# Linear attention and gated MLP, two layers each: block sums of the down weights moved from the first gated MLP into the first attention layer

## The chip, the cores and the metric

The kernel runs on one core of one Trainium2 chip. The metric is the device time of the whole program in microseconds (us), as a median of separate executions; before the change it is 1495.54 us (three runs, 1492.11 to 1496.01). Durations of single instructions come from one further execution that was recorded by the hardware profiler.

TensorE (PE) does the matrix products, VectorE (DVE), ScalarE (ACT) and GpSimd (POOL) the elementwise work, and SyncE (SP) issues most of the transfers. Each engine carries out its own list of instructions in the order of that list[...].

## The reference

Two kinds of layers alternate: attention, MLP, attention, MLP. There are 2048 rows (S) of 1024 numbers (D); the MLP is 3584 wide (F).

```python
# attention layer: 32 heads of 32
qkv = layernorm(x) @ wqkv
pq, pk = phi(q), phi(k)             # t+1 or exp(t), + 1e-6
kv  = sum_s pk[s] v[s]^T ;  z = sum_s pk[s]
x  += ((pq kv) / (pq . z + 1e-6)) @ wo
# gated MLP layer
xn  = layernorm(x)
h   = relu(xn @ W_gate) * (xn @ W_up)
x  += h @ W_down
```

Both attention layers use the same weights, and so do both MLP layers.

## The kernel before

**Attention, `layer_A`.** The 16 row tiles of 128 are taken in four quarters of four tiles. A unit is one projection of one row tile onto 512 columns: 8 matmuls of 128x128 by 512 into one PSUM bank (L430). In the first layer the quarters run as 16 units of quarter 0 (`head_units`), then for q = 1 and q = 2 sixteen units each, in which k and q projections alternate, then the eight k units of quarter 3. After that come the products of the normalised rows with phi(k) (L465), the last q units, and the output units (L557). The banks of the units come from two PSUM pools: four banks of `ps` and, for every third unit outside the last quarter, two of `ps3`; a bank is free again when VectorE has read it (L380, which writes phi). Layernorm of later row tiles goes on beside the units on VectorE: two `bn_stats` of half a row (L154), an aggregate (L159) and the scaling (L168), after which SyncE issues a DMA transpose (L347).

**Gated MLP, `layer_B`.** A layer works in two chunks c of 1024 rows. The gate and up products of one unit u (256 of the 3584 columns; 14 units) are done as a 2x2 block product with seven products instead of eight. Each of the seven is four matmuls (L743), for gate and for up, so a unit has 56 matmuls. This needs sums of blocks of the rows (`sums_x`) and of the weights (`make_gu`, L677 to L680). The sums of the weights are made on VectorE in the first chunk of the first MLP layer only, and stored to DRAM (tensors `tg`, `tu`); later chunks load them. Within a unit the parts are joined on VectorE (L774 and L777: a sum of a PSUM bank and the part m5, one pair for gate, one for up; L754, `put`: times the relu) and POOL (L781). The third product into the bank `yg` (or `yu`) may start only when L774 has read that bank, so a late L774 holds up TensorE.

**Down product, `down`.** The same scheme with seven products of 56 matmuls (L826). It needs sums over h (L805, L806, L808) and sums of blocks of W_down: `make_d(u)` loads four blocks (1 MB, L690), makes four differences (L698 to L701) in place and stores them to the DRAM tensor `td`. It is called for u = 0, 2, ... 12, that is seven times, at the start of every second unit of the first chunk of the first MLP layer. Both chunks of both MLP layers then load `td`.

**What sets the order.** Python emits the work in the order of the PE stream; `later.at(n, f)` emits f after n more ticks, where a tick is one attention unit, half of one block of L465, or one product of a gated unit (14 ticks per unit). The framework's scheduler then arranges the instructions of each engine by priority and by its own idea of when data are there, except inside `manual_schedule` (quarter 0 for VectorE, SyncE and ScalarE; everything from the L465 stage on in an attention layer for VectorE and GpSimd), where the emitted order is kept. `issue_after(i)` keeps a group of instructions behind instruction i. All large buffers (weights in a ring of five, transposed rows, h, and the `wd` tiles of `make_d`) are taken from one pool of 16 slots, so a load waits until a slot is free, and everything behind it on SyncE waits too.

Of the kernel before, what the change touches and what calls it, by code (L numbers as in the profile page):

```python
# [8 lines left out]
ALU = mybir.AluOpType  # L9
# [80 lines left out]
class _Net:  # L90
# [313 lines left out]
    def layer_A(self, l, last_ln):  # L404
        nc, G, KT, D = self.nc, self.G, self.KT, self.D
        ring, later = self.ring, self.later
# [28 lines left out]
        def k_unit(q, j, c, between=None):  # L435
            t = q * QT + j
            pk = self.pk_home(l, t)
            self.phi(project(f"k{c}", q, j, between), pk[:, c * NW:(c + 1) * NW], "v")
            later.at(1 + (10 if self.phi_lag else 0), lambda: k_sum(t, slice(c * NW, (c + 1) * NW)))
# [54 lines left out]
        def q_unit(sc, j, c, lag=None):  # L494
            if c == 0 and (sc, j) not in pq_of:
                a = self.slot(f"pq{l}_{sc}", [P, QT, D])
                for i in range(QT):
                    pq_of[sc, i] = a[:, i, :]
            pq = pq_of[sc, j]
            self.phi(project(f"q{c}", sc, j), pq[:, c * NW:(c + 1) * NW], "s" if sc < self.NQ - 1 else "v")  # L500
            if c == H - 1 and lag is not None:
                later.at(lag, lambda: z_mult(sc, j))
# [65 lines left out]
        def column_major(f, q):  # L568
            return [lambda j=j, c=c: f(q, j, c) for c in range(H) for j in range(QT)]

        def row_major(f, q):
            return [lambda j=j, c=c: f(q, j, c) for j in range(QT) for c in range(H)]

        def run(*lists):

            n = max(len(u) for u in lists)
            for i in range(n):
                for u in lists:
                    if i < len(u):
                        u[i]()  # L580
                        later.tick()
# [7 lines left out]
        if l == 0:  # L589
            first = self.head_units(lambda *a: k_unit(0, *a), lambda *a: q_unit(0, *a), *steps)  # L590
        else:
            first = column_major(k_unit, 0)
# [10 lines left out]
        else:  # L603
            run(first, column_major(q_unit, 0))
        for q in range(1, self.NQ - 1):
            run(row_major(k_unit, q), row_major(q_unit, q))
        run(row_major(k_unit, self.NQ - 1))
        with self.tc.manual_schedule(engines={mybir.EngineType.DVE, mybir.EngineType.Pool}):
# [75 lines left out]
    def make_d(self, u):  # L684

        v = self.nc.vector
        t = self.slot(f"wd{u}", [P, 2, 4, NW])
        T = t[:, :, :, :].bitcast(F16)
        us = slice(u, u + 2)
        self.nc.sync.dma_start(out=t[:, :, :, :].rearrange("p u (h n) f -> p u h (n f)", h=2),  # L690
                               in_=self.wd_v[:, :, us, :].rearrange("p h u n -> p u h n"))

        def behind(fn):
            with self.tc.issue_after(self.last_x.ins):
                fn()

        def sums():
            v.tensor_tensor(out=T[:, :, 0, :], in0=t[:, :, 1, :], in1=t[:, :, 0, :], op=ALU.subtract)  # L698
            v.tensor_tensor(out=T[:, :, 1, :], in0=t[:, :, 3, :], in1=t[:, :, 1, :], op=ALU.subtract)
            v.tensor_tensor(out=T[:, :, 3, :], in0=t[:, :, 3, :], in1=T[:, :, 0, :], op=ALU.subtract)  # L700
            v.tensor_tensor(out=T[:, :, 2, :], in0=t[:, :, 2, :], in1=T[:, :, 3, :], op=ALU.subtract)  # L701
            self.later.at(1, lambda: self.nc.scalar.dma_start(
                out=self.td[:, us, :, :], in_=T))

        self.later.at(4, lambda: behind(sums))

    def sums_x(self, l, c, j):

# [87 lines left out]
    def down(self, l, c, hT, final):  # L796


        nc, later, ring, v = self.nc, self.later, self.ring, self.nc.vector
        N = NW  # L800
        pairs = [(p, [x[:, b::4, :] for b in range(4)]) for p, x in enumerate(hT)]
        e1, e2 = ([self.slot(f"e{i}_{l}_{c}_{k}", dtype=F16) for k in range(2)] for i in (1, 2))
        part = lambda e, p: e[p // 4][:, (p % 4) * 2:(p % 4) * 2 + 2, :]
        for p, (a, _, g, d) in pairs:
            v.tensor_tensor(out=part(e1, p), in0=g, in1=d, op=ALU.add)  # L805
            v.tensor_tensor(out=part(e2, p), in0=part(e1, p), in1=a, op=ALU.subtract)  # L806
        for p, (a, _, g, d) in pairs:
            v.tensor_tensor(out=g, in0=a, in1=g, op=ALU.subtract)  # L808
        raw = lambda b: lambda k: hT[k // 2][:, (k % 2) * 4 + b, :]
        own = lambda e: lambda k: e[k // 8][:, k % 8, :]  # L810
        X = [self.ps.tile([P, N], F32, tag="a", name=f"dx{j}") for j in range(QT)]
        Y = [self.ps3.tile([P, N], F32, tag="b", name=f"dy{j}") for j in range(2)]
        Y += [self.kvp.tile([P, N], F32, tag=f"kv{j}", name=f"dy{2 + j}") for j in range(2)]
        V = []
        t1, t2 = [c * 2 * QT + j for j in range(QT)], [(c * 2 + 1) * QT + j for j in range(QT)]

        def product(p, A, banks, start, done):
            for half in range(2):
                ring.free_before((l, c, p, half))
                w = ring.get((l, c, p, half))  # L820
                w = w if p[0] != "T" else w[:, :, :].bitcast(F16)
                n = self.U // 2
                for j in range(QT):
                    for i in range(n):
                        k = half * n + i
                        nc.tensor.matmul(banks[j], lhsT=A(k)[:, j * P:(j + 1) * P], rhs=w[:, i, :],  # L826
                                         start=start and k == 0, stop=k == self.U - 1,
                                         skip_group_check=True)
                    if half == 1:
                        done(j)  # L830
                    later.tick()

        def seed(j):
            nc.scalar.activation(out=Y[j], in_=X[j], func=ACT.Copy)

        def onto(tiles, n2, banks, last):
            return lambda j: self.add_down(tiles[j], n2 * N, banks[j], final, last)

        product("11", raw(0), X, True, seed)
        product("21", raw(1), X, False, onto(t1, 0, X, True))  # L840
        for p, (_, b, _, _) in pairs:
            v.tensor_tensor(out=b, in0=b, in1=part(e2, p), op=ALU.subtract)
        V = [self.ps.tile([P, N], F32, tag="a", name=f"dv{j}") for j in range(QT)]
        product("T1", own(e1), V, True, onto(t2, 1, V, False))
        product("T2", own(e2), Y, False, onto(t1, 1, Y, False))
        product("T3", raw(2), Y, False, onto(t2, 1, Y, True))

        def first_done(j):
            onto(t1, 1, V, True)(j)
            if not final and t1[j] < self.NS:  # L850
                later.at(1, lambda: self.send_away(t1[j]))

        def second_done(j):
            onto(t2, 0, Y, True)(j)
            if not final and t2[j] < self.NS:
                later.at(1, lambda: self.send_away(t2[j]))

        product("22", raw(1), V, False, first_done)
        product("T4", raw(3), Y, False, second_done)

    def layer_B(self, l, final):
        ring = self.ring

        def behind(it, fn):
            with self.tc.issue_after(it.ins):
                fn()

        for c in range(2):
            hT = []
            first = l == 1 and c == 0  # L870
            for u in range(self.U):
                if u % 2 == 0:
                    hT.append(self.slot(f"h{l}_{c}_{u // 2}", dtype=F16))
                ring.load_to(ring.index((l, c, "g", u)) + 5)
                if first:
                    if u + 1 < self.U:
                        self.later.at(4, lambda u=u: behind(self.last_x, lambda: [
                            self.make_gu(ring.get((l, c, w, u + 1)), w, u + 1) for w in "gu"]))
                if first and u % 2 == 0:
                    self.make_d(u)  # L880
                self.glu(l, c, u, hT)
                if c == 0 and u == (self.U - 1 if first else 0):
                    after = self.last_put.ins
            if c == 0:
                self.ln_chunk(l, 1, 20, 3, 3, after)
            elif not final:
                self.ln_later(l + 1, 0, 28, 6, 4)
            self.down(l, c, hT, final)
# [68 lines left out]
```

## Time and profile before

| | us |
|---|---|
| median of three runs | 1495.54 |
| the profiled execution | 1494.55 |
| its span in the trace | 1492.8 |
| TensorE busy | 1477.1 (99%) |
| VectorE busy | 824.9 (55%) |
| ScalarE busy | 508.1 (34%) |
| GpSimd busy | 275.0 (18%) |

The profiled execution takes 1.7 us more than its span, which is what lies around the recorded instructions. The stages of the span, by the first matmul of each on TensorE:

| stage | from, us | to, us |
|---|---|---|
| attention 1, k and q units | 7.2 | 104.7 |
| attention 1, L465 stage | 104.7 | 163.4 |
| attention 1, last q units and output units | 163.4 | 235.6 |
| MLP 1, chunk 0, gate and up | 235.6 | 416.0 |
| MLP 1, chunk 0, down | 416.0 | 500.8 |
| MLP 1, chunk 1, gate and up | 500.8 | 670.3 |
| MLP 1, chunk 1, down | 670.3 | 754.6 |
| attention 2 | 754.6 | 981.5 |
| MLP 2 | 981.5 | end |

How to read the views that follow. A line of the timeline has the start (us), the duration (us), the engine, the line of the kernel, the operation, what it writes and reads, and how many were merged; in brackets stands how long the engine sat idle just before, and what ended that. A line of the table by stretch has the stretch, its length, then for PE, PEld (weight loads), DVE, ACT and POOL the busy time and number of instructions, then the granted clock of TensorE (1.00 is full), the share of the DMA engines that were busy and what they moved in GB/s.

### The profile page before, as it was taken

The numbers are of one execution on the slowest core, as the hardware profiler recorded it, in microseconds if no ns is written. First come the engines' busy times: TensorE is split into PE (matmuls) and PEld (weight loads), VectorE is DVE, ScalarE is ACT, GpSimd is POOL, SyncE is SP. The second block draws the span as 40 slices with busy tenths as digits, with TensorE's granted clock in tenths as the row PEclk, the third lists the DMA queues.
The fourth block names the chain that finished last, engine by engine and source line by source line (L and its number), as shares of the span: only waits on it lengthen the run. The fifth ranks groups of instructions, "written<-read, shape, count | busy, mean of one in ns | idle before, by whom it ended". The sixth has DMA issues, their size and how long they took to land.

```text
span 1492.8 us, 18537 instructions
## 1 busy us (share of the span) xinstructions
PE 1477.1 (99%) x6993; PEld 670.2 (45%) x7039; DVE 824.9 (55%) x1427; ACT 508.1 (34%) x911; POOL 275.0 (18%) x190
## 2 busy tenths in 40 slices
PE   9999999999999999999999999999999999999999
PEld 4444444444444444444444444444444444444444
DVE  8854589675593544446356545874335433443632
ACT  6751323333340233341057513233332203333300
POOL 1348340101100011110023483401111000111000
PEclk9999999999999999999999999999999999999999
DMA  9502449774658963445823028494444688444461
GB/s 282 99 29 50 100 76 316 252 253 169 221 172 214 349 207 114 142 133 193 244 43 71 29 50 252 78 279 143 133 150 136 185 239 282 141 141 141 149 210 43
DMA packets 313754, 242.92 MB, mean 163 GB/s; under 512 B 105280, under 2 KB 290880, under 8 KB 312768
## 3 DMA queue, kind: packets, MB, share of 16 engines
q1 hardware_dynamic: 302688, 214.07, 49.4%
q10 hardware_dynamic: 10976, 27.66, 4.9%
q8 instruction: 55, 0.90, 0.2%
q14 instruction: 35, 0.29, 0.1%
HBM read 186.65 MB, written 30.41 MB: 145 GB/s over the span
## 4 chain that ended last, share of the span: by engine, by line
PE 92%; DVE 3%; DMA 3%; issue 1%; ACT 0%; DVEq 0%
PE ps L430 15%; PE dy L826 10%; PE yu L743 9%; PE yg L743 9%; PE ps L465 7%; PE dv L826 6%; PE dx L826 6%; PE xg L743 6%; PE xu L743 6%; PE ps L557 5%; PE zu L743 3%; PE zg L743 3%; PE vu L743 3%; PE vg L743 3%; DMA wd<-in_B_W_down_dram 2%
## 5 line engine op out<-in xcount | busy, mean ns | idle before, releaser
L743 PEld LDWEIGHTS <-w 128*128 128x128 f16 (+1 forms) x3136 | 306.6, 98 | 381.6 <-issue 12.9
L781 POOL TENSOR_TENSOR h<-m5u,m5g 128x512 f16<-128x512 f32 x56 | 73.1, 1305 | 820.7 <-DVE m5u L777 787.3
L430 PE MATMUL ps<-w,xnT 128*128 128x512 bf16 x1024 | 223.5, 379 | 0.2 <-ACT xnT L291 0.2
L826 PEld LDWEIGHTS <-h 128*128 128x128 f16 x1120 | 109.5, 98 | 132.3
L430 PEld LDWEIGHTS <-xnT 128*128 128x128 bf16 x1024 | 99.3, 98 | 120.1 <-issue 1.6
L774 DVE TENSOR_TENSOR zg<-yg,m5g 128x512 f32<-128x512 f32 x56 | 39.1, 698 | 203.2 <-PE yg L743 199.0
L743 PE MATMUL yu<-s,w 128*128 128x512 f16 x448 | 115.3, 380 | 3.9 <-DVE zu L774 3.9
L743 PE MATMUL yg<-s,w 128*128 128x512 f16 x448 | 115.3, 379 | 3.3 <-DVE zg L774 3.2
L743 PE MATMUL xu<-xnT,w 128*128 128x512 f16 x448 | 115.0, 379 | 0.1
L743 PE MATMUL xg<-xnT,w 128*128 128x512 f16 x448 | 115.0, 379 | 0.0
L557 PE MATMUL ps<-T,pqT 128*128 128x512 bf16 x500 | 110.4, 379 | 1.4 <-DVE x L564 0.8
L751 ACT ACTIVATE m5g<-m5g 128x512 f32<-128x512 f32 x56 | 35.2, 629 | 192.6 <-DVE m5g L777 182.8
L826 PE MATMUL dy<-w,h 128*128 128x512 f16 x448 | 98.0, 379 | 0.0
L826 PE MATMUL dx<-w,h 128*128 128x512 bf16 x436 | 96.7, 379 | 0.6
L511 POOL TENSOR_TENSOR kvc<-pq,kvc 128x1024 f32<-128x1024 bf16 x32 | 68.0, 2124 | 84.5 <-DVE den L516 71.1
L557 PEld LDWEIGHTS <-pqT 128*128 128x128 bf16 x512 | 49.9, 98 | 61.4 <-issue 1.5
L154 DVE BATCH_NORM_STATS2 stats<-x 128x6 f32<-128x512 f32 (+1 forms) x120 | 76.3, 671 | 0.6 <-DMA x<-in_A_x_dram 0.3
L380 DVE SCALAR_TENSOR_TENSOR pq<-ps,e 128x512 bf16<-128x512 f32 x64 | 43.9, 686 | 49.0 <-ACT e L374 46.8
L161 ACT ACTIVATE rstd<-mv,eps 128x1 f32<-128x1 f32 x64 | 18.0, 289 | 155.3 <-DVE mv L159 155.1
L516 DVE TENSOR_REDUCE den<-kvc 128x32 f32<-128x1024 f32 x32 | 38.9, 1214 | 54.1 <-POOL kvc L511 54.1
L447 POOL TENSOR_TENSOR kvc<-kvc,slab 128x512 f32<-128x512 f32 x46 | 53.9, 1180 | 78.3 <-DVE slab L380 61.0
L826 PEld LDWEIGHTS <-e 128*128 128x128 f16 x448 | 43.8, 98 | 52.9
(105 smaller groups left out, 1923.0 us busy)
## 6 DMA issues: line engine op xcount, KB each, us to landing
w<-in_B_W_gate_dram SPq DMA_DIRECT2D x56, 512.0 KB, 6.0
w<-in_B_W_up_dram SPq DMA_DIRECT2D x56, 512.0 KB, 5.0
w<-td SPq DMA_DIRECT2D x32, 896.0 KB, 4.6
w<-in_B_W_down_dram SPq DMA_DIRECT2D x24, 896.0 KB, 5.1
w<-tg SPq DMA_DIRECT2D x42, 512.0 KB, 6.9
w<-tu SPq DMA_DIRECT2D x42, 512.0 KB, 6.0
w<-in_A_wqkv_dram SPq DMA_DIRECT2D x10, 1024.0 KB, 8.0
wd<-in_B_W_down_dram SPq DMA_DIRECT2D x7, 1024.0 KB, 6.4
```

The costliest lines, as they stand in the source:

```text
L154: self.nc.vector.bn_stats(out=stats[:, c, :], in_=src[:, c * fmax:(c + 1) * fmax])
L380: nc.vector.scalar_tensor_tensor(out=out, in0=ps, scalar=0.0, in1=e, op0=ALU.max, op1=ALU.add)
L430: nc.tensor.matmul(by_row(ps), lhsT=self.xnT[l, l_q][:, kt, j * P:(j + 1) * P], rhs=w[:, kt, :].rearrange("p (b i d) -> p i b d", i=R, d=H ...
L447: nc.gpsimd.tensor_tensor(out=ksum[:, cols], in0=ksum[:, cols], in1=pk, op=ALU.add)
L465: nc.tensor.matmul(ps, lhsT=self.xn[l, t][:, d * P:(d + 1) * P], rhs=self.pk[l, t][:, h * NW:(h + 1) * NW], start=(t == 0), stop=(t == sel ...
L511: nc.gpsimd.tensor_tensor(out=prod, in0=pq_of[sc, j], in1=zrow, op=ALU.mult)
L516: nc.vector.tensor_reduce(out=den, in_=heads(prod), axis=mybir.AxisListType.X, op=ALU.add)
L557: nc.tensor.matmul(ps, lhsT=pqT[sc][:, g, j * P:(j + 1) * P], rhs=T[g // 4][:, g % 4, n2 * NW:(n2 + 1) * NW], start=(g == 0), stop=(g == G ...
L743: nc.tensor.matmul(ps, lhsT=W[w][m][:, k, :], rhs=A[m][:, k, :], start=start and k == 0, stop=k == 3, skip_group_check=True)
L774: nc.vector.tensor_tensor(out=Z[w], in0=Y[w], in1=V[w], op=ALU.add)
L781: nc.gpsimd.tensor_tensor(out=h[:, 3, :], in0=V["u"], in1=V["g"], op=ALU.mult)
L826: nc.tensor.matmul(banks[j], lhsT=A(k)[:, j * P:(j + 1) * P], rhs=w[:, i, :], start=start and k == 0, stop=k == self.U - 1, skip_group_che ...
```

## The change

It has three parts. `make_d` is no longer called in the gated units; its seven calls are put into the first attention layer, from the start of q = 1 on, eight ticks apart. The four differences follow the load by six ticks (four before) without an `issue_after`, and their store follows by two ticks on SyncE's queue (one tick, on ScalarE's queue, before). In all four down products the sums over h are put behind the last `put` of the gated units.

```diff
@@ layer_A
         for q in range(1, self.NQ - 1):
+            if (l, q) == (0, 1):
+                for i in range(self.U // 2):
+                    later.at(1 + 8 * i, lambda i=i: self.make_d(2 * i))
             run(row_major(k_unit, q), row_major(q_unit, q))
@@ make_d
-        def behind(fn):
-            with self.tc.issue_after(self.last_x.ins):
-                fn()
-
         def sums():
...
-            self.later.at(1, lambda: self.nc.scalar.dma_start(
+            self.later.at(2, lambda: self.nc.sync.dma_start(
                 out=self.td[:, us, :, :], in_=T))
 
-        self.later.at(4, lambda: behind(sums))
+        self.later.at(6, sums)
@@ down
-        for p, (a, _, g, d) in pairs:
-            v.tensor_tensor(out=part(e1, p), in0=g, in1=d, op=ALU.add)
-            v.tensor_tensor(out=part(e2, p), in0=part(e1, p), in1=a, op=ALU.subtract)
-        for p, (a, _, g, d) in pairs:
-            v.tensor_tensor(out=g, in0=a, in1=g, op=ALU.subtract)
+        with self.tc.issue_after(self.last_put.ins):
+            for p, (a, _, g, d) in pairs:
+                v.tensor_tensor(out=part(e1, p), in0=g, in1=d, op=ALU.add)
+                v.tensor_tensor(out=part(e2, p), in0=part(e1, p), in1=a, op=ALU.subtract)
+            for p, (a, _, g, d) in pairs:
+                v.tensor_tensor(out=g, in0=a, in1=g, op=ALU.subtract)
@@ layer_B
-                if first and u % 2 == 0:
-                    self.make_d(u)
                 self.glu(l, c, u, hT)
```

In the program built from the changed code, TensorE's list is the same up to the first gated unit, and in that chunk a few groups of matmuls change places: the first unit is no longer mixed with parts of the second.

## The prediction

> **What bounds the kernel now.** First the busy times: TensorE is all but full, so only its gaps and slow spells can be won.
>
> ```profile
> PE 1477.1 (99%) x6993; PEld 670.2 (45%) x7039; DVE 824.9 (55%) x1427; ACT 508.1 (34%) x911; POOL 275.0 (18%) x190
> ```
>
> Then the table by stretches of 25 us, to see where they lie. A stretch at full rate holds 116 to 118 matmuls; the worst two hold 99 and 100, both in the first gated chunk, the one in which `make_d` runs. The last line is the same work in chunk 1, without it.
>
> ```profile
> 325.00:350.00 25.00, 22.69 (x99) 9.80 (x97) 14.18 (x24) 7.80 (x14) 2.42 (x2) 0.93 0.61 208
> 350.00:375.00 25.00, 21.78 (x100) 9.64 (x99) 14.94 (x27) 7.97 (x14) 1.38 (x2) 1.00 0.48 168
> ...
> 575.00:600.00 25.00, 25.00 (x118) 11.32 (x116) 9.71 (x14) 9.92 (x17) 2.54 (x2) 1.00 0.42 135
> ```
>
> By its first and last matmul chunk 0 takes 416.0 - 235.6 = 180.4 us, chunk 1 takes 670.3 - 500.8 = 169.5: 10.9 us are lost in the former. TensorE's timeline names the losses:
>
> ```profile
> 330.07 1.03 PE L743 MATMUL zg<-s,w 128*128 128x512 f16 x4
> 333.40 1.31 PE L743 MATMUL yu<-s,w 128*128 128x512 f16 x4 [2.31 <-DVE zu L774]
> 334.51 1.91 PE L743 MATMUL zu<-s,w 128*128 128x512 f16 x4
> 336.22 1.62 PE L743 MATMUL yg<-xnT,w 128*128 128x512 f16 x4
> ...
> 359.40 1.02 PE L743 MATMUL yg<-s,w 128*128 128x512 f16 x4 [1.71 <-DVE zg L774]
> ```
>
> All wait for L774 on VectorE. VectorE's timeline tells why L774 was late: ahead of it in the list stood a sum whose load had not landed.
>
> ```profile
> 330.85 0.69 DVE L698 TENSOR_TENSOR wd<-wd 128x1024 f16<-128x1024 bf16 x1 [2.62 <-DMA wd<-in_B_W_down_dram]
> 357.13 0.69 DVE L677 TENSOR_TENSOR w<-w 128x1024 f16<-128x1024 bf16 x1 [1.84 <-DMA w<-in_B_W_gate_dram]
> 370.35 0.69 DVE L698 TENSOR_TENSOR wd<-wd 128x1024 f16<-128x1024 bf16 x1 [4.81 <-DMA wd<-in_B_W_down_dram]
> 399.15 0.69 DVE L698 TENSOR_TENSOR wd<-wd 128x1024 f16<-128x1024 bf16 x1 [2.12 <-DMA wd<-in_B_W_down_dram]
> ```
>
> Groups of four matmuls start 0.86 us apart; what exceeds that is loss. wd at 331: 333.40 - 330.07 - 0.86 = 2.47, and the next groups, at half clock, start 1.11, 1.71 and 1.46 apart, 1.70 more: 4.17. Gate load at 357: 1.87. wd at 371 and 374: 1.16 + 0.68 = 1.84. Gate loads at 385 and 387: 0.53. wd at 400: 0.99. Gaps between 243 and 268, while VectorE works off sums of gate, up and down weights: 1.0. Start of the chunk, waiting for the first gate sums: 0.40. Sum 10.8 of the 10.9.
>
> Last, the place that receives the work: VectorE while quarters 1 and 2 are projected.
>
> ```profile
> 45.00:50.00 5.00, 5.00 (x25) 2.24 (x23) 5.00 (x11) 3.27 (x8) 3.05 (x3) 1.00 0.63 63
> 55.00:60.00 5.00, 5.00 (x25) 2.25 (x23) 5.00 (x12) 3.19 (x7) 1.16 (x1) 1.00 0.57 106
> 75.00:80.00 5.00, 5.00 (x25) 2.25 (x23) 2.64 (x5) 3.51 (x6) 1.45 (x2) 1.00 0.00 0
> ```
>
> It is full up to 60 us (third busy figure, 5.00 of 5) and half idle from 70 on; TensorE doesn't notice, since PSUM banks buffer it.
>
> [...] L378, 0.42 us alone, took 1.36 when it met a POOL add.
>
> ```profile
> 94.86 1.15 POOL L447 TENSOR_TENSOR kvc<-kvc,slab 128x512 f32<-128x512 f32 x1 [2.30 <-DVE slab L380]
> 94.93 1.36 DVE L378 TENSOR_SCALAR e<-e 128x512 f32<-128x512 f32 x1 [0.22 <-ACT e L370]
> ```
>
> [...] the gate load issued at 350.60 beside others landed after 6.5 us, that of 321.41 within 3.9 (its sum began at 325.27). [...] Here 2.3 us of idling were enough (granted clock 0.50 in 334 to 336), 1.7 us were not.
>
> **The change part by part.**
>
> *`make_d` leaves the gated chunk.* With it go its seven loads, 28 sums (L698 to L701, about 0.71 us each, 20 us of VectorE) and seven stores. The three wd stalls go: 4.17 + 1.84 + 0.99 = 7.0 us. In the first two units the list of the changed program brings L774 forward: in the old one L698, L699 and a gate sum stood before it, and it started at 243.28; without them it starts at 241.74, ends by 242.4, and its matmul is due at 243.0. So the gaps of 243 to 268 (1.0) go too; the 0.40 stays, as the first gate sum stays first.
>
> *What is late next.* In the changed list the gate and up loads still wait for the slots of units four and five back, and their sums stand three units ahead of use. In unit 9 the pair u(11), g(12) is again issued at the end of unit 8, 0.86 us apart, and both stand before unit 9's L774: that 1.87 stays. In unit 11 the pair g(13), u(13) now stands the same way, where before one of the two stood after L774 (0.53). I price that between 0.4 (the pair lands in 5.0 us, with less traffic beside it) and 1.9 (as in unit 9), and take 1.3. In unit 7 only one load, g(10), is that late, and lands in 3.9 us as at 321.41, in time. So here 7.0 + 1.0 + 0.53 - 1.3 = 7.2 us are won.
>
> *The sums arrive in attention.* TensorE waits only if VectorE reads a bank too late. A unit takes 8 x 0.216 = 1.73 us; six banks rotate, so a bank is needed again five units (8.6 us) after its unit ended, and its read (0.69) must start within 7.9. The 40 units after quarter 0 end at 104.6, so the fifth of q = 1 ended at 44.1, and its read started at 48.50: lag 4.4; the worst one was 5.2. The built list puts eight sums (wd0, wd2) between units 5 and 12 of q = 1, and moves layernorm statistics behind them. Adding that list up from 47.15 with the spacings of the trace (read 0.60, L378 0.34, L168 0.46, L154 0.60, sum 0.65) the reads fall at 48.8, 51.2, 52.8, 54.9, 56.3, 58.2, 59.8, 62.1, 63.8: a lag of at most 5.8. POOL is busy about 40% of that time (8.3 of the 20 us from 40 to 60); if such a share of sums waits half a POOL add (0.6 us), eight sums take 2 us more: 7.8, just within. wd4 and wd6 fall where VectorE is half idle. wd8 falls among the k units of quarter 3, where four banks allow 4.5 us; the lag there is 1.9 (read at 101.32, unit ended 99.4), with four sums 4.5. wd10 and wd12 come in the L465 stage, which doesn't need VectorE's results; POOL's chain of L511 and L523 may slip by some us, but its first quarter is needed only at 179 and done by about 139. Bounds 0 and 3 us, value 0.5.
>
> *Loads and stores on SyncE.* Fourteen issues join. The load of wd0 follows the transpose at 37.96 + 1.23 = 39.2 and lands after 6.4 us (row median) to 8.6 (the one of 322.28): 45.6 to 47.8, while its first sum is due at 48.1. A store waits for its last sum, and behind the first stores stand transposes of row tiles 11 to 13. Tile 11 went at 52.5 and is needed by its unit at 83; so up to 30 us of waiting cost nothing. The load of v's second half, behind wd8's, moves from 64 to about 91 and lands by about 100; it is used at about 115. Value 0. ScalarE loses seven issues of 0.33 us, which nobody waited for: 0.
>
> *Sums over h behind the last `put`.* 21 sums of 0.60 us, 12.6 us, start when the chunk ends instead of 6 us before. First needed are e1's, two products of 12.1 us later; the nearer reader is the L894 that frees the first bank, and the list puts four statistics fewer before it, so it moves from 20.8 to about 21.8 us after the chunk's end, with 24.2 allowed. In the other three chunks nothing stalls now (a stretch at a joint lacks at most 0.16 us of 25). Between -0.5 and +0.7 us; value 0.
>
> Sum: 7.2 - 0.5 = 6.7. The profiled execution, 1494.55, becomes 1487.9 (span 1486.1); the median lies 1.0 above it, so 1488.8.
>
> **Rivals.**
>
> *VectorE binds in attention (slower).* If every sum of q = 1 and of quarter 3 meets POOL and takes about 1.44 us, as L700 did at 260.81, then in q = 1 the lag is 5.8 + 8 x 0.79 = 12.1, so TensorE waits 4.2 and 1.7 more at half clock; in quarter 3 it is 1.9 + 4 x 1.35 = 7.3, so 2.8 + 1.7. Together 10.4 against 7.2 won: 1498.7. It decides from about 1.2 us per sum. For it: VectorE is full up to 60 us. Against it: POOL is busy less than half the time, and most L378 there still took 0.42.
>
> *The gate pairs take over.* If in units 9 and 11 the wait passes 2.3 us and the clock halves, each costs 4.17: 8.5 - 0.5 - (4.17 - 1.87) - 4.17 = 1.5 won, 1494.0. For it: both pairs have sums ahead of their data. Against it: 1 MB less per two units in each direction moves beside them.
>
> *It does nothing.* The sums of gate and up weights wait in wd's stead wherever wd waited: 1495.0. Against it: at 371 and 400 no gate load was due.
>
> **How the numbers follow.** Forecast 0.72, its own range 1486 to 1491 (each unknown at its ends); pairs 0.15; nothing 0.06; VectorE 0.07. A measurement of this kernel tells 0.3%, 4.5 us, from no change. Faster by that: 0.73; within: 0.19; slower: 0.08. The range takes in the pairs' case, and the low end all unknowns at their best: 1485.5 to 1494.0.
>
> **What would show it.** No wd row after 235 us; the stretch 325 to 350 at 116 or more matmuls; the first gated chunk in about 173 us; one wait of about 1.8 us for L774 in unit 9 and one in unit 11; no TensorE wait on L380 between 40 and 105 us. I am wrong if TensorE waits there, or if a half-clock spell appears in the chunk.

## The result, and the profile after

| | before | after |
|---|---|---|
| median, us | 1494.95 (6 runs, 1492.11 to 1497.46) | 1490.33 (6 runs, 1489.03 to 1492.36) |
| profiled execution / its span | 1494.55 / 1492.8 | 1490.50 / 1488.6 |

The ratio is 0.9971, 95% interval 0.9957 to 0.9985: faster, by 0.3%, which is 4.3 us (2.2 to 6.4). The forecast was 6.7 us faster, to 1488.8. In the changed file the lines have moved: L743 is L742 now, L774 is L773, L777 is L776, the gate and up sums are L680 to L683, the differences of the down weights L697 to L700.

The page's busy times of after:

```profile
PE 1474.4 (99%) x6993; PEld 670.5 (45%) x7039; DVE 836.7 (56%) x1427; ACT 508.6 (34%) x911; POOL 277.1 (19%) x190
```

They say as little as those of before, since TensorE is all but full in both. The table by stretch, over the first gated chunk of after, says more. Its columns are those of before:

```profile
325.00:350.00 25.00, 25.00 (x118) 11.33 (x116) 15.09 (x27) 9.94 (x18) 2.54 (x2) 1.00 0.47 154
350.00:375.00 25.00, 23.48 (x110) 10.57 (x109) 14.10 (x23) 8.70 (x16) 2.54 (x2) 1.00 0.39 136
375.00:400.00 25.00, 22.89 (x107) 10.28 (x106) 12.49 (x20) 8.27 (x15) 2.54 (x2) 1.00 0.37 128
```

The stretch that held 99 matmuls holds 118. Two stretches still lack 8 to 11. TensorE's timeline of after has one wait in each, in units 9 and 11:

```profile
352.95 1.03 PE L742 MATMUL yu<-s,w 128*128 128x512 f16 x4
355.50 1.02 PE L742 MATMUL yg<-s,w 128*128 128x512 f16 x4 [1.52 <-DVE zg L773]
...
378.59 1.03 PE L742 MATMUL yu<-s,w 128*128 128x512 f16 x4
381.73 1.02 PE L742 MATMUL yg<-s,w 128*128 128x512 f16 x4 [2.11 <-DVE zg L773]
```

Four matmuls take 0.86 us from start to start, so 355.50 - 352.95 - 0.86 = 1.69 us are lost at the first place and 2.28 us at the second. VectorE's timeline of after shows why, for the second: sums of gate and of up weights, each waiting for its load, stand ahead of L773. Two such sums ahead of one read are called a gate pair from here on.

```profile
375.96 0.69 DVE L680 TENSOR_TENSOR w<-w 128x1024 f16<-128x1024 bf16 x1 [2.38 <-DMA w<-in_B_W_gate_dram]
379.45 0.69 DVE L680 TENSOR_TENSOR w<-w 128x1024 f16<-128x1024 bf16 x1 [1.88 <-DMA w<-in_B_W_up_dram]
380.98 0.69 DVE L773 TENSOR_TENSOR zg<-yg,m5g 128x512 f32<-128x512 f32 x1
```

In attention VectorE is now nearly full from 45 to 105 us (third busy figure), where it was half idle from 70 us on:

```profile
55.00:60.00 5.00, 5.00 (x25) 2.29 (x24) 5.00 (x12) 4.28 (x11) 2.67 (x2) 1.00 0.70 246
75.00:80.00 5.00, 5.00 (x25) 2.23 (x24) 4.86 (x9) 4.87 (x9) 1.47 (x1) 1.00 0.84 166
```

and TensorE waited for it in this execution, as the view shows twice:

```profile
65.27 14.98 PE L430 MATMUL ps<-w,xnT 128*128 128x512 bf16 x68 [0.20 <-DVE pq L380]
...
109.28 1.02 PE L465 MATMUL ps<-slab,x 128*128 128x512 bf16 x4 [0.47 <-DVE slab L380]
```

Counted from start to start these cost 0.37 and 0.64 us. A third one, of 0.13 us of idling at 86.4 us (0.29 lost), is too short for the view to mark; it too ended with a read of L380.

TensorE's list is nearly the same in both programs, so the starts of the stages give an account of the two traces. The last column is the lead of after.

| TensorE reaches | before | after | lead |
|---|---|---|---|
| first projection beyond the start | 9.38 | 9.54 | -0.16 |
| first gated chunk | 235.60 | 237.22 | -1.62 |
| its down product | 416.04 | 411.08 | +4.96 |
| second attention layer | 754.46 | 749.50 | +4.96 |
| second MLP | 981.50 | 977.30 | +4.20 |
| last down product | 1404.55 | 1400.35 | +4.20 |

So attention lost 1.46 us, the chunk won 6.58 (180.44 to 173.86 us), and 0.76 went again at the joint, the place where the second attention layer ends and the second MLP begins; the first product there waited 0.73 us for the last `sums_x`.

### The profile page after: what moved, and what is told of

Read it like the earlier page. It is cut to its first block, busy times and chain, and to the rows that moved or that the text cites. A ratio compares the mean times of both kernels' runs of the same rounds, so it can differ in the third digit from the quotient of the medians.

```text
span 1488.6 us, 18556 instructions
## 1 busy us (share of the span) xinstructions
PE 1474.4 (99%) x6993; PEld 670.5 (45%) x7039; DVE 836.7 (56%) x1427; ACT 508.6 (34%) x911; POOL 277.1 (19%) x190
## 4 chain that ended last, share of the span: by engine, by line
PE 85%; DVE 5%; DMA 2%; issue 1%; ACT 0%; DVEq 0%
PE dy L826 10%; PE yu L742 10%; PE yg L742 10%; PE ps L430 8%; PE ps L465 7%; PE dv L826 6%; PE dx L826 6%; PE xu L742 6%; PE xg L742 6%; PE zu L742 3%; PE zg L742 3%; PE vu L742 3%; PE vg L742 3%; PE ps L557 2%; DVE x L564 1%; DVE stats L154 1%
## 5 line engine op out<-in xcount | busy, mean ns | idle before, releaser
L742 PEld LDWEIGHTS <-w 128*128 128x128 f16 (+1 forms) x3136 | 306.6, 98 | 375.8 <-issue 4.6
L773 DVE TENSOR_TENSOR zg<-yg,m5g 128x512 f32<-128x512 f32 x56 | 39.1, 699 | 210.9 <-PE yg L742 210.9
L742 PE MATMUL yg<-s,w 128*128 128x512 f16 x448 | 115.1, 379 | 3.6 <-DVE zg L773 3.6
L742 PE MATMUL xu<-xnT,w 128*128 128x512 f16 x448 | 115.0, 379 | 0.0
L742 PE MATMUL xg<-xnT,w 128*128 128x512 f16 x448 | 115.0, 379 | 0.0
L742 PE MATMUL yu<-s,w 128*128 128x512 f16 x448 | 115.0, 379 | 0.0
L511 POOL TENSOR_TENSOR kvc<-pq,kvc 128x1024 f32<-128x1024 bf16 x32 | 68.1, 2129 | 81.5 <-DVE den L516 70.4
L447 POOL TENSOR_TENSOR kvc<-kvc,slab 128x512 f32<-128x512 f32 x46 | 57.1, 1249 | 78.8 <-DVE slab L380 61.0
L759 ACT ACTIVATE m5g<-vg 128x512 f32<-128x512 f32 x56 | 33.4, 597 | 100.6 <-PE vg L742 73.9
L776 DVE TENSOR_TENSOR m5u<-yu,m5u 128x512 f32<-128x512 f32 x56 | 38.7, 691 | 50.7 <-PE yu L742 50.7
```

Source lines behind the costliest of these rows:

```text
L447: nc.gpsimd.tensor_tensor(out=ksum[:, cols], in0=ksum[:, cols], in1=pk, op=ALU.add)
L511: nc.gpsimd.tensor_tensor(out=prod, in0=pq_of[sc, j], in1=zrow, op=ALU.mult)
L742: nc.tensor.matmul(ps, lhsT=W[w][m][:, k, :], rhs=A[m][:, k, :], start=start and k == 0, stop=k == 3, skip_group_check=True)
L773: nc.vector.tensor_tensor(out=Z[w], in0=Y[w], in1=V[w], op=ALU.add)
L776: nc.vector.tensor_tensor(out=V[w], in0=Y[w], in1=V[w], op=ALU.add)
```

## The experiments

In the order in which they ran. Each ratio is to before, from the same chip and hour; before itself had medians of 1492.44 (36 runs), 1493.63 (51) and 1494.15 us (27) beside the three groups, so read the ratios. A ratio given here is not the quotient of the two medians (in experiment 7 that would be 0.9942 and not 0.9952), but the quotient lies within the interval each time.

**1. The third part alone, on before.** The edit is the third part of the diff, nothing else.

> Before, with the third part of the change alone: the sums over h of the four down products behind the last put; the sums of the down weights stay in the gated chunk. My theory: this part is worth nothing (the chunk ends and the down products begin as before), so 1495 us within 0.5 us, ratio 1.000. Rival: it carries part of the change's gain or loss (for example the 0.76 us that the trace of after lacks at the joint from the second attention layer to the second MLP); then the ratio leaves 1.000 by 0.0005 or more and the gated chunk's length differs from 180.4 us.

1493.98 us (14 runs); ratio 1.001 (0.9999 to 1.0021): no gain, and at most 3 us of loss. Both marks of the rival came, a ratio 0.001 away and a chunk that is not 180.4 us long, but the interval takes in 1.000, and a shorter chunk is no loss. The trace taught something else. Up to the last unit of the first gated chunk VectorE has the list of before here, and yet the chunk took 411.45 - 235.89 = 175.56 us, not 180.44. TensorE's timeline at the place of the worst wait of before:

```profile
333.20 1.02 PE L743 MATMUL yu<-s,w 128*128 128x512 f16 x4 [1.87 <-DVE zu L774]
334.06 1.03 PE L743 MATMUL zu<-s,w 128*128 128x512 f16 x4
```

The load of wd8 landed a little earlier (VectorE stood 2.17 us for it, not 2.62), TensorE idled 1.87 us instead of 2.31, and no spell at half clock followed (the next groups start 0.86 us apart). All waits behind wd here come to 0.38 + 2.03 + 0.67 = 3.1 us (the idle times 0.22, 1.87 and 0.51 with the 0.16 by which the modelled ends overlap); in the trace of before the prediction counted 7.0, and with a wait at 306 us that it left out they are 7.45. The joint before the second MLP cost 0.42 here, with the sums of attention not moved.

**2. After, without the sums of the down weights.**

```diff
-                for i in range(self.U // 2):
-                    later.at(1 + 8 * i, lambda i=i: self.make_d(2 * i))
...
-                        src = self.td[:, us, self.T_AT[p], :]
+                        src = self.wd_v[:, self.T_AT[p] % 2, us, ...]
```

> After, without the sums of the down weights anywhere: no load, difference or store of them; the down products read plain blocks of the weights in place of td, transfers of the same size. The output is thus not the reference's. The time shows what the seven calls cost in the first attention layer. My theory: attention lasts as before (first gated matmul at 235.6 instead of 237.2) and the gated chunk as in after (173.9), so 1.4 us less than after, about 1488.9. Rival 1: the 1.6 us come from somewhere else (start of the program, order of the list), then attention stays at 237 and the time at 1490.3. Rival 2: the stores or the loads also slow the gated chunk, then it falls below 173 us.

This kernel leaves the sums out, so its output is not the reference's. 1487.64 us (9 runs); ratio 0.9967 (0.9956 to 0.9978), against 0.9971 and 0.9977 for after: the sums in attention cost between nothing and 2 us. My 1.4 us are not confirmed: the first gated matmul came at 236.47, and from the first projection (9.49) to there the trace has 226.98 us, longer than a second trace of after (experiment 8, 226.64). Of these, 0.47 us went at 11.7 us, where TensorE waited for the first weights, ahead of all that was changed; without that the two differ by 0.13. The chunk took 171.91 us. That is under the 173 of my second rival, but the second trace of after, with all the stores and loads, has 172.37.

**3. After, with the gate and up sums nearer to their use.**

```diff
-                        self.later.at(4, lambda u=u: behind(self.last_x, lambda: [
+                        self.later.at(4, lambda u=u: behind(self.last_put if u else self.last_x, lambda: [
```

> After, with each unit's sums of gate and up weights kept behind the last put of the unit before the one in which they are asked for, so that they stand one unit ahead of use instead of up to three. My theory: the two waits left in the gated chunk (1.69 us in unit 9 and 2.28 in unit 11) come only from sums queued ahead of their data on VectorE, and vanish: the chunk takes 170 us, the program 4.0 us less than after, about 1486.3. Rival: VectorE then has six sums (4 us) to do between a unit's last put and its first L774 (here L773), is late with it in every unit, and TensorE waits a little in each: 14 times 0.3 us or more, and the time does not fall.

1484.92 us (5 runs, 1484.80 to 1487.06); ratio 0.9953 (0.9939 to 0.9966). The theory holds, and the rival does not: the chunk takes 406.06 - 236.30 = 169.76 us, near the 669.86 - 500.64 = 169.22 of chunk 1 in before, and the two stretches with waits are full:

```profile
350.00:375.00 25.00, 25.00 (x118) 11.29 (x117) 14.80 (x26) 9.93 (x17) 2.54 (x2) 1.00 0.48 159
375.00:400.00 25.00, 25.00 (x117) 11.35 (x116) 12.84 (x21) 9.33 (x16) 2.54 (x2) 1.00 0.51 182
```

**4. Before, with the differences left in the chunk but a unit later.**

```diff
-            with self.tc.issue_after(self.last_x.ins):
+            with self.tc.issue_after(self.last_put.ins):
...
-        self.later.at(4, lambda: behind(sums))
+        self.later.at(18, lambda: behind(sums))
```

> Before, with the seven calls where they were, but their differences 14 ticks (one unit) later and behind the last put: the same loads, differences and stores in the same chunk, only no longer queued ahead of their data. My theory: the 7.0 us of waits for wd come from the order of VectorE's list alone, so they vanish here too, attention costs nothing, and the gate waits stay (1.9 and 0.5, perhaps 1.9 each): about 1495.0 - 7.0 + 0 to 1.4 = 1488 to 1489.4. Rival: it is the 20 us of differences and the 14 MB of transfers within the chunk that cost the time; then it stays at 1493 or above, the waits turning up at the gate sums or at L774 behind a difference.

1488.43 us (18 runs); ratio 0.9976 (0.9969 to 0.9983). The theory holds. No wait for a load of wd is left in the trace, with all 28 differences, loads and stores still in the chunk. This is the size of the whole change (0.9971 and 0.9977), without moving anything out of the MLP. What stays is a gate pair in unit 9 with 2.33 us of idling and a spell at half clock, and 0.80 us of idling at 392 us, where an activation stood on ScalarE behind the store of a late sum of up weights.

**5. After, with the calls at other places in attention.**

```diff
-                    later.at(1 + 8 * i, lambda i=i: self.make_d(2 * i))
+                    later.at((15, 19, 23, 27, 38, 44, 50)[i], lambda i=i: self.make_d(2 * i))
```

> After, with the seven calls at other places of the first attention layer: ticks 15, 19, 23, 27, 38, 44 and 50 instead of 1, 9, 17, ... 49, so that the differences fall into the second half of q = 1, q = 2 and the L465 stage, and no longer into the first half of q = 1 and quarter 3. My theory: the waits on L380 in the trace of after (0.36 us at 65, 0.63 at 109) are late reads of PSUM behind the differences, and vanish: attention from its first projection to the first gated matmul takes 226.3 us as in before (227.7 in after, 226.6 in the run of the later gate sums, which has the same list here), so 0.4 to 1.4 us less than after. Rival: those waits came from where loads and GpSimd's adds happened to fall in one execution; then the time is that of after within 0.3 us. Rival 2: the chain on GpSimd in the L465 stage slips further, and TensorE waits for pqT after 180.

1492.32 us (14 runs); ratio 0.9992 (0.9982 to 1.0003). The theory was wrong, and each of the rivals too: about 2 to 3 us slower than after. Attention took 240.85 - 9.87 = 230.98 us, 4.34 more than in experiment 8. VectorE's timeline, then TensorE's:

```profile
94.89 0.69 DVE L697 TENSOR_TENSOR wd<-wd 128x1024 f16<-128x1024 bf16 x1 [1.92 <-DMA wd<-in_B_W_down_dram]
```

```profile
100.53 8.75 PE L430 MATMUL ps<-w,xnT 128*128 128x512 bf16 x32 [2.41 <-DVE slab L380]
```

A difference stood ahead of its data again, now in attention. SyncE's queue shows where the load was: behind two stores that waited for their differences.

```profile
81.44 5.84 SPq L701 DMA_DIRECT2D td<-wd  x2
87.33 4.28 SPq L693 DMA_DIRECT2D wd<-in_B_W_down_dram  x2
```

VectorE stood still for 1.92 us, was still behind at 100 us, and TensorE ran out of banks. The wait cost 2.57 us from start to start, and a spell at half clock that followed it (100.61 to 104.02 us) 1.7 more: together nearly all of the 4.34.

**6. Experiments 3 and 5 together.**

> After, with both edits: the gate and up sums one unit ahead of use, and the seven calls at the other ticks. My theory: what is left of waits is the start and 1.0 us at the joint of attention to the MLP; 0.4 to 1.0 us less than with the later gate sums alone, which was 7.0 us (0.9953) below before: ratio 0.9946 to 0.9951. Rival: attention has nothing left to give, ratio 0.9953 as with the gate sums alone.

1489.48 us (21 runs); ratio 0.9976 (0.9967 to 0.9984), 0.23% (3.4 us) slower than experiment 3 alone, so neither the theory nor the rival came. The trace repeats the wait of 2.41 us at 100.63 behind the same late load, this time without a spell at half clock, and has one of 0.92 at 111.85; the chunk is clean. The loss by the bad places and the gain by the gate order add up.

**7. Before, with both orders mended and nothing moved.** The edits of 3 and 4 in before.

> Before, with nothing moved to attention: the differences of the down weights one unit later and behind the last put, and the gate and up sums behind the last put of the unit before. My theory: what counted was the order of VectorE's list and not the place of the work, so all waits for L774 but some 0.3 us each in the first two units vanish here as well, and attention costs nothing: 7 to 8 us below before, ratio 0.9947 to 0.9953. Rival: 20 us more of VectorE's work in the chunk, ten sums (6.8 us) in a row in every second unit, make L774 late without any load being late: seven units with 0.5 us or more, ratio 0.997 or above.

1484.92 us (6 runs, 1484.56 to 1485.18); ratio 0.9952 (0.9937 to 0.9967). The theory holds, and the rival does not. TensorE waits for nothing in the chunk after its first unit; it takes 405.79 - 236.04 = 169.75 us, with VectorE at 17.90 us of 25 instead of 14.80 (third busy figure):

```profile
350.00:375.00 25.00, 25.00 (x118) 11.31 (x116) 17.90 (x32) 9.55 (x17) 2.54 (x2) 1.00 0.69 238
```

The ratio of experiment 3 (0.9953), with the work in the other place and without the third part. That the medians agree to the hundredth is chance, as they come from different chips.

**8. After once more.**

> After once more, unchanged, beside the three others. My theory: the waits for loads differ from execution to execution (the trace of before showed 7.0 us of waits for wd, that of the same chunk with the third part alone 2.4 us), so this trace shows other waits than the first one: the gate pairs in units 9 and 11 again, 1 to 2.3 us each, attention between 226.5 and 227.7 us; the time 4.3 us (0.9971) below before, within 0.5. Rival: the waits are fixed by the list, and the trace repeats 1.69, 2.28, 0.36 and 0.63 us to a tenth.

1489.25 us (22 runs); ratio 0.9977 (0.9969 to 0.9985). Attention took 236.03 - 9.39 = 226.64 us, with one wait on L380 that the view doesn't mark (0.27 us lost at 108 us); the gate pairs cost 0.42 and 2.06 us; the chunk took 172.37; at the joint to the second MLP TensorE idled 0.88. The rival is out, and the theory holds in kind but not in its bounds: 0.42 lies under 1 us, and 0.9977 is 3.4 us and not 4.3 within 0.5. The waits stand at the same places of the list as in the first trace and differ in length: ahead of the second sum of unit 9's pair VectorE stood 1.68 us for the load there and 0.43 here. The list sets where a wait can be; the landing of a load sets how long it is.

**9. After, with the stores on ScalarE's queue.**

```diff
-            self.later.at(2, lambda: self.nc.sync.dma_start(
+            self.later.at(2, lambda: self.nc.scalar.dma_start(
```

> After, with the stores of the down weights' sums left on ScalarE's queue, where before had them. Each store waits for its last difference, and behind it on ScalarE stand the activations of the next units, which read PSUM for phi; the scheduler also puts the differences of the second call four in a row, ahead of the reads of L380. My theory: ScalarE waits for VectorE at the first two stores (VectorE is full up to 68 us and some 6 us behind), so phi of the next units and with it L380 come late and TensorE waits for a bank: 2 to 6 us slower than after, all of it between 45 and 75 us. Rival: ScalarE, a third busy, takes it up, and the time is that of after within 1 us; then the change of queue was worth nothing.

1502.55 us (6 runs); ratio 1.0066 (1.0052 to 1.0080): some 13 us slower than after, more than twice what I expected. All of it lies in attention, which took 250.13 - 9.67 = 240.46 us. The direction of the theory was right, the place was not: the waits reach to 142 us. ScalarE's timeline at the first store, and at the last:

```profile
53.42 0.34 ACTq L701 DMA_DIRECT2D td<-wd  x1
53.81 0.63 ACT L373 ACTIVATE e<-e 128x512 f32<-128x512 f32 x1 [3.62 <-DVE wd L700]
...
141.64 1.08 ACT L470 ACTIVATE mt<-ps 128x512 bf16<-128x512 f32 x2 [11.89 <-DVE wd L700]
```

In the L465 stage VectorE's list holds the differences behind the sums of L516, which wait for GpSimd; the store waits for the last difference, and the copy of the finished bank (L470) stands behind the store. TensorE idled 6.04 us for it, and 2.1 us more went at half clock after that. I had looked for the cost only where VectorE is full.

**10. Before, with only the gate order mended.** The edit of 3 in before.

> Before, with only the gate and up sums kept behind the last put of the unit before; the differences of the down weights stay where they were, ahead of their data. With the runs of before, of the late differences and of both this makes a table of two by two. My theory: the two kinds of waits add up, so about half of the 8.7 us between before (1493.6) and both (1484.9) comes back: 1489 to 1491, and the trace shows waits for wd (L698) at units 7, 9 and 11 and none for gate or up. Rival: the waits for wd grow where the gate sums no longer stand ahead of them (the same late load is waited for in another place), and the time stays at 1493.

1490.56 us (22 runs); ratio 0.9974 (0.9965 to 0.9982). With before, experiment 4 and experiment 7 this makes the table:

| ratio to before | gate and up sums early | one unit ahead |
|---|---|---|
| differences of wd early | 1 | 0.9974 |
| differences a unit later | 0.9976 | 0.9952 |

The theory holds within the intervals: 0.26% and 0.24% alone, 0.48% together. The time did not stay at that of before, as the rival has it. The waits for wd stay in this trace, at 332 us for example:

```profile
332.27 1.02 PE L743 MATMUL yu<-s,w 128*128 128x512 f16 x4 [2.07 <-DVE zu L774]
```

They cost some 5.7 us in this one execution, between the 3.1 of experiment 1 and the 7.45 of before, so whether they grow a little without the gate sums ahead of them can't be told from single traces.

**11. After, with every difference doubled.** Behind each of the four stands a second operation on its result.

```diff
             v.tensor_tensor(out=T[:, :, 0, :], in0=t[:, :, 1, :], in1=t[:, :, 0, :], op=ALU.subtract)
+            v.tensor_tensor(out=T[:, :, 0, :], in0=T[:, :, 0, :], in1=T[:, :, 0, :], op=ALU.max)
```

> After, with each of the 28 differences followed by an operation of the same size that leaves its result as it is (the maximum of the block with itself): twice the work for VectorE in attention, nothing else. It tests the point from which the rival of the prediction decides, 1.2 us per sum. My theory: by the prediction's sum the lag of L380 in q = 1 becomes 5.8 + 8 x 0.65 = 11.0 against 7.9 allowed, and in quarter 3 4.5 + 4 x 0.65 = 7.1 against 4.5: TensorE waits 3.1 and 2.6 us there and some 1.7 more each at half clock, 5 to 9 us slower than after, that is at or above before. Rival: VectorE takes it up where it is half idle, and the time is within 1.5 us of after.

1502.54 us (6 runs); ratio 1.0068 (1.0050 to 1.0086), some 13 us slower than after, which is more than the 5 to 9 expected. TensorE waits for L380 from 73 us on, eight times, most at

```profile
101.30 3.61 PE L430 MATMUL ps<-w,xnT 128*128 128x512 bf16 x16 [2.41 <-DVE pq L380]
...
119.00 3.18 PE L465 MATMUL ps<-slab,x 128*128 128x512 bf16 x14 [3.18 <-DVE slab L380]
```

Attention takes 247.82 - 9.46 = 238.36 us, 11.7 more than in experiment 8. None of the eight waits lies in q = 1, which ends at about 63 us (eleven units of 1.73 us behind the 44.1 us of the prediction) and where the prediction's sum had the largest one; they come in q = 2, where before left VectorE half idle, and after it. So a rival that I gave 7 in 100 begins less than a factor of two away: VectorE has room for the 28 differences in attention, and not for 56.

## Why the prediction was right, and where it was off

*The mechanism, right.* What is won comes from the first gated chunk, by the waits for wd that go. Experiments 4, 7 and 10 sharpen it: it is the order of VectorE's list, not the place of the work. A sum that stands in the list ahead of its data holds up everything behind it (the one at 331 us in before stood 2.62 us for its load, with L774 behind it); 28 differences more in the same chunk cost nothing when they stand behind their loads (experiments 3 and 7). Attention was never needed for it.

*"The three wd stalls go: 4.17 + 1.84 + 0.99 = 7.0 us."* This is the term that was mis-sized. The 7.0 were read from one execution, in which the wait at 331 grew to 2.31 us and 1.70 us of half clock followed. One wait behind wd is missing in them, at 306 us. In VectorE's timeline of before a difference stands still for its load:

```profile
303.23 0.69 DVE L698 TENSOR_TENSOR wd<-wd 128x1024 f16<-128x1024 bf16 x1 [0.69 <-DMA wd<-in_B_W_down_dram]
```

and in TensorE's the third product waits for the L774 behind it:

```profile
306.98 1.02 PE L743 MATMUL yu<-s,w 128*128 128x512 f16 x4 [0.29 <-DVE zu L774]
```

It cost 0.45 us. The count of 10.8 seemed to leave no room for it because chunk 1 was put at 169.5 us; by the first matmuls its stage runs from 500.64 to 669.86 us (the stage table has 500.8 and 670.3), which is 169.22, so 11.2 us were to be explained. The same list in experiment 1 had 3.1 us where this trace has 7.45. The medians of many executions give 0.24% (3.6 us) for these waits when the work stays in the chunk (experiment 4), and 0.22% (3.3 us) between experiments 10 and 7, where the gate order is mended in both. The prediction moved the sum by 1.0 us to reach the median and left this term at its one reading; 1.70 of it hung on a spell that the other execution didn't have. That the waits vary is shown. A second reason stays open: when the waits for wd go, the gate pairs may wait longer in their stead, as in the trace of experiment 4, and the medians can't part the two.

*Gate pairs.* Unit 9 was put at 1.87 us: 1.69, then 0.42. Unit 11 was put at 1.3 between 0.4 and 1.9: 2.28, then 2.06, above the bound. I took 6.5 us as the longest landing from one row; one trace gives no bound for a wait for a load. The sum of both, 3.17, lies between the measured 3.97 and 2.48. The rival in which these pairs fall to half clock did not come in either trace of after, but in experiment 5 one of 2.08 us did, so it deserved its chance; the length of the 2.11 us in after didn't rule it out (see the last section).

*Attention 0.5 us (0 to 3).* It cost 1.46 us in the first trace; from the first projection to the first gated matmul it took 226.64 and 226.63 us (experiments 8 and 3) against 226.2 to 226.6 in the runs with nothing moved (before, experiments 1, 4, 7 and 10), so it cost 0.0 to 0.4 there. "Just within" was what it was: in one trace of three L380 came late at 65 and 86 us (0.37 and 0.29 us lost). The prediction had said that it was wrong if TensorE waited there, so by its own sign it failed on this point, by 0.7 us. The place was off too: I had the least room in q = 1, where none of the eight sums took more than 0.68 us in the first trace of after. The late reads came later, at 65, 86 and 109 us, each close behind a VectorE instruction that had run beside an add of GpSimd and took longer than others of its line (L168 with 1.38 us and not 0.54, L699 with 1.53 and L700 with 1.64 and not 0.68). That these caused the waits was not tested.

*Loads and stores on SyncE: 0.* Right for the calls as they are placed. Experiment 5 shows how narrow it is, since two stores that waited for VectorE held back the next load there (81.44 to 87.33 us), and experiment 9 what the change of queue was worth. I called ScalarE's seven issues "0" and didn't ask what the stores would have cost there in attention: 13 us.

*Sums over h behind the last `put`: 0.* Within -0.1 and +3 us by experiment 1; experiments 3 (with it) and 7 (without it) both have 1484.92. The 0.76 us at the joint to the second MLP, which no step had foreseen, isn't its work: 0.36 in experiment 4 without the third part, none in experiments 2 and 6 with it, 0.88 in experiment 8. It follows the landing of the last transposed tile; why that varies was not tested.

*The sum.* It was 7.2 - 0.5 = 6.7 by the forecast; it came to 6.58 - 1.46 - 0.76 - 0.16 = 4.20 in the two traces, and to 4.3 (0.9971) and 3.4 (0.9977) in the medians. That the traces nearly agree with the forecast in the chunk (6.58 to 7.2) is in part luck. Two errors of the sum work against each other: with the wait left out (0.45) it would have been 7.7, and with the gate pairs at their measured 3.97 in place of 3.17 it would then be 6.9; of the gaps between 243 and 268 us, 0.24 stayed, which leaves 6.6 beside the measured 6.58. And both traces are single executions of something that varies: the chunk took 180.44 us in this one of before and 175.56 in experiment 1, 173.86 in this one of after and then 172.37. The execution of before was no outlier in total (1494.55, beside a median of 1494.95); that of experiment 1, with 1490.41, was the fastest of its 14.

*A better version.* Experiments 3 and 7 take 1484.92 us and beat both kernels; all 6 runs of experiment 7 lie below all 22 of after from the same chip and hour (from 1487.85 on). Their runs also lie closer: 1484.56 to 1485.18 in experiment 7, where before has 1489.51 to 1498.81 (51 runs) beside it, and 1484.80 to 1487.06 in the 5 of experiment 3. With the waits for late loads most of the scatter goes too, as far as so few runs can tell.

## What to carry to other kernels

When TensorE waits for an engine, look at what stands ahead in that engine's list. If it is an instruction that waits for a load, moving it a little later in the same list was worth as much here as moving the work to another stage, and cost nothing elsewhere. Before a wait is priced, ask how it varies: the landing of a transfer differs from execution to execution, and two traces of the same list differed here by almost 5 us in one chunk. A DMA that waits for a result belongs on a queue behind which nothing urgent stands: the same store cost nothing to speak of on SyncE as after has it, 2 to 3 us where it held back the next load (experiment 5), and 13 us on ScalarE.

## What the runs showed of the hardware

*The clock after a gap.* The length of a gap did not by itself decide whether TensorE's granted clock fell; the prediction's 2.3 us that were enough, and 1.7 that were not, are those of its one trace. After 2.08 us (experiment 5, unit 11), 2.31 (before) and 2.33 us (experiment 4) TensorE ran at half clock for a while; after 2.33 (experiment 9, at 369 us) and even 3.18 us (experiment 11, at 119 us) it did not; and 2.41 us at 100.6 us were followed by a spell in experiment 5 and by none in experiment 6.

The spells of before (334.00 to 337.41 us) and of experiment 5 (100.61 to 104.02 and 383.92 to 387.33 us) last 3.41 us each, at a granted clock of 0.50; the one after the 6.04 us of experiment 9 lasts an estimated 6.8 us, by the clock of the stretches there (0.67 from 139 to 142 us, 0.50 to 145, 0.70 to 148). Here are the two spells of experiment 5, each with the 3.41 us ahead of it, in which its gap lies. TensorE's busy time is the first figure behind the length, and the granted clock is the third from the end:

```profile
97.20:100.61 3.41, 1.00 (x6) 0.37 (x4) 3.41 (x6) 0.60 (x1) 0.59 (x1) 1.00 0.01 3
100.61:104.02 3.41, 3.41 (x9) 1.22 (x9) 3.10 (x6) 0.00 (x0) 3.40 (x3) 0.50 0.75 308
...
380.51:383.92 3.41, 1.33 (x7) 0.56 (x6) 2.33 (x5) 0.00 (x0) 0.00 (x0) 1.00 0.40 157
383.92:387.33 3.41, 3.41 (x9) 1.18 (x8) 1.71 (x3) 0.63 (x1) 0.00 (x0) 0.50 0.38 154
```

In before the 3.41 us ahead of the spell hold 1.10 us of TensorE's work (6 matmuls). And here is the longer gap of experiment 11, 115.82 to 119.00 us, with the clock at 1.00 throughout:

```profile
114.25:117.66 3.41, 1.57 (x8) 0.59 (x6) 3.41 (x4) 0.00 (x0) 1.91 (x2) 1.00 1.08 363
117.66:121.08 3.42, 2.08 (x10) 0.97 (x10) 3.42 (x6) 0.60 (x1) 1.47 (x1) 1.00 0.42 154
121.08:124.49 3.41, 3.41 (x17) 1.47 (x15) 3.38 (x5) 0.81 (x1) 1.47 (x1) 1.00 0.32 132
```

Why the clock fell behind some gaps and not behind others was not shown. Behind the gap of 2.11 us in after, 379.62 to 381.73 us, it stayed at 1.00, with 17 matmuls from 384.49 to 387.90 us.

One spell of 3.41 us, with work throughout, costs 1.7 us: it holds 9 matmuls in experiment 5, and as long a stretch at full clock 17 in experiment 11, eight more of 0.216 us.

*A difference beside a GpSimd instruction.* A difference alone takes 0.68 us. In the first trace of after it took 1.53 to 1.64 us when it began beside an add of GpSimd's (L447), and 2.28 and 2.29 us in the L465 stage, beside L511 and L523. Whatever their length, each ended 0.54 to 0.55 us after the GpSimd instruction that it had met.
